# X by tokens from VectorE's 32 by 32 turns and a round trip through DRAM, in place of TensorE's transposes, in 13 of 14 chunks

## The chip, the cores and the metric

The program runs on one core of a Trainium2 chip. The metric is device microseconds (us) of one execution. Each comparison is made of several executions of both kernels, and their medians are compared; one more execution is taken by the hardware profiler, and all rows below come from it.

## The reference

Three layers follow each other: an attention with a sigmoid, a mixer with a low-rank token product and a two-layer channel product, and a second mixer. Only the last one is touched by the change. Cut to that:

```python
def _moe2_ref(x, w_theta, w_tok_r, w_tok_i, w_ch):   # x: 4 batches x 448 tokens x 768 features
    theta = x @ w_theta
    zr = x * np.cos(theta)
    zi = x * np.sin(theta)
    y = np.einsum('ts,bsd->btd', w_tok_r, zr) + np.einsum('ts,bsd->btd', w_tok_i, zi)
    u = x + y
    return u + np.maximum(u @ w_ch, 0.0)
```

## The kernel before

**Layout.** X lies in SBUF for the whole kernel as `X[P, NK, NT]`: 128 features on the partitions, 6 groups of features, 4 x 448 = 1792 tokens along the free axis. Each product is made of three matmuls on pairs of a high and a low part (`uh`/`ul`, `gh`/`gl`, `xh`/`xl`, `zh`/`zl`). The high part is a ScalarE copy, the low part a subtraction on VectorE (`lo_dve`, L119) or GpSimd (`lo_pool`, L113).

**The channel loop.** For `i` in 12 blocks of hidden channels and `b` in 4 batches, `ch1(i, b)` (36 matmuls of 448 columns) is followed by `ch2` of the pair before (three parts `e2`, 12 matmuls each). Behind each part VectorE adds the result `y` from PSUM to X (L690), and `y` has two PSUM buffers. `hook(i, b)` is called after each part, and runs one step of a conversion of a later weight (`tick`). The low part `gl` (L672) is also made by VectorE. The last block is `i == L` (11); in it a batch of X is complete after its third addition. In this block SyncE's queue also loads `tok` (the 3.1 MB of token weights, L749), the theta weights `th_r` (L236) that were kept in DRAM, and stores the last converted weights (L231).

**The theta stage.** The 1792 tokens are cut into 14 chunks of 128. For chunk `c`, `project` (L799, L800, L803) makes theta with tokens on the partitions in one of two PSUM buffers `th`; `trig` reduces it with two VectorE instructions (L819, L820) into the tile `t1`, and ScalarE makes sine and cosine in `t2` and `t1`, which have two buffers each. Since theta has tokens on the partitions, X is wanted with tokens on the partitions too. `natural` makes this: six TensorE transposes of 128 x 128 (L811) with the identity `ident` write one chunk of X into the PSUM tile `xn`. `zmake` (or `zmul` for the last chunk) multiplies it by sine and cosine on VectorE (L854, L856; L864, L865 in the two chunks that span two batches), then `zsplit` makes high and low parts, and the low parts are made by GpSimd for most chunks. `split_x` prepares `xh` and `xl` of the chunk after next, also with two buffers. `zmake` of one chunk stands in the middle of the next chunk's `project`. After chunks 4, 7 and 13 a `mix` of a batch follows (126 matmuls of 448 columns), whose `y` has two PSUM buffers that VectorE adds to X (L881).

**Order.** The schedule is manual: on each engine the instructions stand in the order in which the code issues them, and each engine runs its own in order. A DMA stands in the queue of the engine that issues it, and waits there for its data and its buffer. Buffers of a pool that are used again wait for their last reader.

Of the kernel before, what the change touches and what calls it, by code (L numbers as in the profile page):

```python
# [24 lines left out]
def tile_kernel(  # L25
# [59 lines left out]

    dpool = ctx.enter_context(tc.tile_pool(name="dpool", bufs=1, space=bass.MemoryType.DRAM))

    ident = cpool.tile([P, P], F32, name="ident")
    bias_s = cpool.tile([P, 1], F32, name="bias_s")
    half_pi = cpool.tile([P, 1], F32, name="half_pi")  # L90
    X = cpool.tile([P, NK, NT], F32, name="X")
# [9 lines left out]
    def pool(name, side="left", space=None):  # L101
        st = ExitStack()
        kw = dict(name=name, bufs=1, side=side, reuse_waits="tile")
        if space is not None:
            kw["space"] = space
        return st.enter_context(tc.tile_pool(**kw)), st
# [104 lines left out]

    kept = {}
    tok_d = dpool.tile([P, 2, NZ, S], F32, name="tok_d")

    def spill_tile(name):
        return late["sp"].tile([P, 2 * DM], F32, tag="sp", name=f"sp_{name}", bufs=1)
# [82 lines left out]
    ap, ap_st = pool("ap")  # L299
    ap1, ap1_st = pool("ap1")  # L300
    ap2, ap2_st = pool("ap2")
    ps_a, ps_a_st = pool("ps_a", "left", PSUM)
    ps_b, ps_b_st = pool("ps_b", "right", PSUM)
    u_in = ap.tile([P, 2, NS, R], F32, name="u_in")
# [407 lines left out]

    u23, u23_st = pool("u23")
    ps_y, ps_y_st = pool("ps_y", "left", PSUM)
    def hook(i, b):
        def after(e2):
            if (i, b) == (0, 1):
                ps = ps_g.tile([P, FB, 512], F32, tag="g", name=f"hl_{e2}", bufs=2)
                U2(B - 1, 2 * e2, ps, (vhl, vll))
            if i == 0 and b in (1, 2):  # L720
                split_u(b + 1, u23, 2 * e2, 2 * e2 + 2, lo_pool)
            tick(i, b, e2 + 2)
        return after
# [15 lines left out]
    for i in range(NB):  # L739
        for b in range(B):  # L740
            tick(i, b, 0)
            if (i, b) not in ((0, 0), (0, 1)):
                ch1(i, b)
            if i == L and b == 1:
                u01_st.close()
                tokhl, tokhl_st = pool("tokhl", "right")
                ctx.enter_context(tokhl_st)
                tok = tokhl.tile([P, 2, NZ, S], F32R, name="tok")
                nc.sync.dma_start(out=f(tok), in_=tok_d)  # L749
                tok_h, tok_l = tok[:, 0], tok[:, 1]  # L750
                xr, xr_st = pool("xr", "right")
                ctx.enter_context(xr_st)
            if i == L and b >= 2:
                split_x(b - 2)
            if i == L and b == 0:
                th_t[0] = load_kept("th0", "w1")
            if i == L and b == B - 1:
                th_t[2] = load_kept("th2", "w1")
                th_t[3] = load_kept("th3", "w1")
            if i == L and b == 1:  # L760
                th_t[1] = load_kept("th1", "w2")
            tick(i, b, 1)
            if prev is not None:
                ch2(*prev, hook(i, b))
            prev = (i, b)
            if (i, b) == (0, 1):
                uv_st.close()
                late["sp"], sp_st = pool("sp")
# [2 lines left out]
    th_t[4] = load_kept("th4", "w2")  # L771
    th_t[5] = load_kept("th5", "w2")
    sp_st.close()
    u23_st.close()
    gpool_st.close()
    cv_st.close()
# [26 lines left out]
                nc.tensor.matmul(ps[:, j, :HN], l[:, kk, :], wh[:, sl], start=False, stop=kk == NK - 1)  # L803
        return ps[:, :, :HN]

    def natural(c, name):

        ps = ps_e.tile([P, 2, 512], F32, tag="xn", name=f"{name}_{c}")
        for kk in range(NK):
            j, o = divmod(kk * P, HN)  # L810
            nc.tensor.transpose(ps[:, j, o:o + P], X[:, kk, c * P:(c + 1) * P], ident)  # L811
        return ps[:, :, :HN]

    def trig(c):

# [10 lines left out]
    def zsplit(key, t, lo):  # L826
        h = zp.tile([P, 2, HN], F32R, tag="zh", name=f"zh_{key[0]}_{key[1]}", bufs=12)
        l = zp.tile([P, 2, HN], F32R, tag="zl", name=f"zl_{key[0]}_{key[1]}", bufs=12)
        hi_act(h, t)
        lo(l, t, h)  # L830
        z_t[key] = (h.rearrange("p a n -> p (a n)"), l.rearrange("p a n -> p (a n)"))
# [4 lines left out]

    def zmul(c):
        cos, sin = T_t[c]
        xn = natural(c, "xn")
        nc.vector.tensor_mul(sin, xn, sin)  # L840
        nc.vector.tensor_mul(cos, xn, cos)

# [6 lines left out]
    def zmake(c):  # L849
        pr, ci, b, i = where(c)  # L850
        if ci != NFULL:
            cos, sin = T_t.pop(c)
            xn = natural(c, "xn")
            nc.vector.tensor_mul(sin, xn, sin)  # L854
            zsplit((b, NFULL + i), sin, lo_pool)
            nc.vector.tensor_mul(cos, xn, cos)  # L856
            zsplit((b, i), cos, lo_pool)
        else:
            cos, sin = T_t.pop(c)
            xn = natural(c, "xn")  # L860
            for n in range(2):
                t = zp.tile([P, 2, HN], F32, tag="zr", name=f"zr_{c}_{n}", bufs=2)
                sl = slice(n * REM, (n + 1) * REM)
                nc.vector.tensor_mul(t[REM:], xn[sl], sin[sl])  # L864
                nc.vector.tensor_mul(t[:REM], xn[sl], cos[sl])  # L865
                zsplit((2 * pr + n, 2 * NFULL), t, lo_pool if n else lo_dve)

    def mix(b, after=None):
        for d in range(NK):
# [12 lines left out]
            if after is not None:  # L882
                after(d)

    project(0, th_t, "th", 0, 4)
    project(1, th_t, "th", 0, 4)
    for c in range(NTC):
# [107 lines left out]
```

## Time and profile before

| what | value |
|---|---|
| median of 3 runs (lowest, highest) | 1170.18 us (1169.7, 1170.59) |
| the profiled execution, its own time | 1170.08 us |
| its span, first to last instruction | 1168.3 us |
| TensorE matmuls busy | 1155.3 us (99%) |
| VectorE, ScalarE, GpSimd busy | 647.9, 360.9, 189.5 us |
| mean granted TensorE clock | 0.998 |

Busy times are unions of an engine's instructions; matmuls overlap each other, so a busy TensorE is not one at its peak. In the rows of a timeline the first number is the start in us from the span's start, the second the duration, and a bracket at the end gives the idle time before it and who ended it. PE is TensorE, DVE is VectorE, ACT is ScalarE, POOL is GpSimd, SPq is the queue of SyncE.

### The profile page before, as it was taken

The numbers are of one execution on the slowest core, as the hardware profiler recorded it, in microseconds if no ns is written. First come the engines' busy times: TensorE is split into PE (matmuls) and PEld (weight loads), VectorE is DVE, ScalarE is ACT, GpSimd is POOL, SyncE is SP. The second block draws the span as 40 slices with busy tenths as digits, with TensorE's granted clock in tenths as the row PEclk, the third lists the DMA queues.
The fourth block names the chain that finished last, engine by engine and source line by source line (L and its number), as shares of the span: only waits on it lengthen the run. The fifth ranks groups of instructions, "written<-read, shape, count | busy, mean of one in ns | idle before, by whom it ended". The sixth has DMA issues, their size and how long they took to land.

```text
span 1168.3 us, 15638 instructions
## 1 busy us (share of the span) xinstructions
PE 1155.3 (99%) x6414; PEld 1000.5 (86%) x6414; DVE 647.9 (55%) x805; ACT 360.9 (31%) x465; POOL 189.5 (16%) x136
## 2 busy tenths in 40 slices
PE   7999999999999999999999999999999999999998
PEld 3444458999999999999999999999999999999997
DVE  4777873445554555455545556565375542732443
ACT  5878872212221222122212222222125341630110
POOL 2300012211111111111111122222002321410000
PEclk9999999999999999999999999999999999999999
DMA  9887830113231323132313242424431000120444
GB/s 168 165 162 141 161 83 1 55 54 97 51 133 54 97 52 131 54 97 53 130 54 98 66 140 61 155 61 156 164 138 52 1 1 1 45 119 1 61 64 66
DMA packets 183719, 100.57 MB, mean 86 GB/s; under 512 B 151232, under 2 KB 174656, under 8 KB 183520
## 3 DMA queue, kind: packets, MB, share of 16 engines
q1 hardware_dynamic: 156800, 87.95, 28.3%
q0 software_dynamic: 2368, 8.24, 2.5%
q10 hardware_dynamic: 24480, 3.39, 2.0%
q8 instruction: 50, 0.82, 0.3%
q14 instruction: 21, 0.17, 0.0%
HBM read 81.40 MB, written 18.15 MB: 85 GB/s over the span
## 4 chain that ended last, share of the span: by engine, by line
PE 97%; DMA 1%; SPq 1%; DVE 1%; ACT 0%; issue 0%; ACTq 0%
PE g L664 10%; PE g L666 10%; PE g L665 10%; PE y L686 10%; PE y L688 10%; PE y L687 10%; PE av L419 5%; PE sc L393 4%; PE y L877 3%; PE y L876 3%; PE y L878 3%; PE th L799 3%; PE th L803 3%; PE th L800 2%; PE wc L958 2%; PE wc L959 2%
## 5 line engine op out<-in xcount | busy, mean ns | idle before, releaser
L690 DVE TENSOR_TENSOR X<-y,X 128x896 f32<-128x896 f32 x144 | 157.1, 1091 | 114.9 <-PE y L688 113.5
L686 PE MATMUL y<-gh,w 128*128 128x448 f32 x576 | 210.7, 366 | 0.2 <-DVE X L690 0.2
L664 PE MATMUL g<-uh,w 128*128 128x448 f32 x576 | 210.7, 366 | 0.0
L687 PE MATMUL y<-gl,w 128*128 128x448 f32 x576 | 210.4, 365 | 0.0
L688 PE MATMUL y<-gh,w 128*128 128x448 f32 x576 | 210.4, 365 | 0.0
L666 PE MATMUL g<-uh,w 128*128 128x448 f32 x576 | 210.4, 365 | 0.0
L665 PE MATMUL g<-ul,w 128*128 128x448 f32 x576 | 210.4, 365 | 0.0
L671 ACT ACTIVATE gh<-g 128x896 fp32r<-128x896 f32 x48 | 44.1, 919 | 390.8 <-PE g L666 390.8
L672 DVE SCALAR_TENSOR_TENSOR gl<-g,gh 128x896 fp32r<-128x896 f32 x48 | 52.4, 1092 | 183.8 <-ACT gh L671 183.8
L113 POOL TENSOR_TENSOR w<-ca_w,w 128x768 fp32r<-128x768 f32 x42 | 77.8, 1853 | 432.0 <-ACT w L110 432.0
L664 PEld LDWEIGHTS g<-uh,w 128*128 128x128 f32 x576 | 108.2, 188 | 9.8 <-ACT uh L110 0.7
L686 PEld LDWEIGHTS y<-gh,w 128*128 128x128 f32 x576 | 108.2, 188 | 9.7 <-issue 1.1
L688 PEld LDWEIGHTS y<-gh,w 128*128 128x128 f32 x576 | 108.2, 188 | 8.6
L666 PEld LDWEIGHTS g<-uh,w 128*128 128x128 f32 x576 | 108.2, 188 | 8.6
L687 PEld LDWEIGHTS y<-gl,w 128*128 128x128 f32 x576 | 108.2, 188 | 8.6
L665 PEld LDWEIGHTS g<-ul,w 128*128 128x128 f32 x576 | 108.2, 188 | 8.5
L384 ACT ACTIVATE A<-sc,bias_s 128x896 f32<-128x896 f32 x72 | 72.2, 1006 | 23.4 <-PE sc L393 12.8
L419 PE MATMUL av<-A,v 128*64 128x448 f32 x288 | 65.2, 561 | 0.0
L876 PE MATMUL y<-tok,zh 128*128 128x448 f32 x168 | 61.7, 367 | 0.0
L877 PE MATMUL y<-tok,zh 128*128 128x448 f32 x168 | 61.5, 366 | 0.0
L113 POOL TENSOR_TENSOR zl<-t,zh 128x768 fp32r<-128x768 f32 x23 | 42.7, 1880 | 115.4 <-ACT zh L110 115.4
L878 PE MATMUL y<-tok,zl 128*128 128x448 f32 x168 | 61.4, 366 | 0.0
(139 smaller groups left out, 1634.6 us busy)
## 6 DMA issues: line engine op xcount, KB each, us to landing
ws_w<-in_moe_w_ch_dram SPq DMA_DIRECT2D x40, 768.0 KB, 4.4
ws_w<-in_moe_w_ch_dram POOLq DMA_DIRECT2D x8, 768.0 KB, 5.9
k<-in_k_dram SPq DMA_DIRECT2D x94, 56.0 KB, 2.7
q<-in_q_dram SPq DMA_DIRECT2D x93, 56.0 KB, 3.1
ws_th<-in_moe_w_theta_dram SPq DMA_DIRECT2D x6, 768.0 KB, 4.3
th_d<-sp_th SPq DMA_DIRECT2D x6, 768.0 KB, 4.1
ws_wc<-in_moe_w_ch_dram SPq DMA_DIRECT2D x6, 768.0 KB, 4.7
wc_d<-sp_wc SPq DMA_DIRECT2D x6, 768.0 KB, 4.5
```

The lines of the kernel that those rows point to most:

```text
L113: nc.gpsimd.tensor_sub(o, a, b)
L419: nc.tensor.matmul(ps[h * D:(h + 1) * D, :S], v_t[p // 2][:, 2 * (p % 2) + h, c, :], A_t[p, c][:, h, :], start=c == 0 and p % 2 == 0, stop ...
L664: nc.tensor.matmul(o, wh[:, sl], uh_t[b][:, kk, :], start=kk == 0, stop=False)
L665: nc.tensor.matmul(o, wh[:, sl], ul_t[b][:, kk, :], start=False, stop=False)
L666: nc.tensor.matmul(o, wl[:, sl], uh_t[b][:, kk, :], start=False, stop=kk == NK - 1)
L686: nc.tensor.matmul(o, wh[:, sl], gh[:, j, :], start=j == 0, stop=False)
L687: nc.tensor.matmul(o, wh[:, sl], gl[:, j, :], start=False, stop=False)
L688: nc.tensor.matmul(o, wl[:, sl], gh[:, j, :], start=False, stop=j == FB - 1)
L690: nc.vector.tensor_add(x, ps[:, :, :S], x)
L876: nc.tensor.matmul(o, zh[:, sl], tok_h[:, i, :], start=n == 0, stop=False)
L877: nc.tensor.matmul(o, zh[:, sl], tok_l[:, i, :], start=False, stop=False)
L878: nc.tensor.matmul(o, zl[:, sl], tok_h[:, i, :], start=False, stop=n == NZ - 1)
```

## The change

The transposes leave TensorE for chunks 0 to 12. In their place each batch of X, once complete, is turned by VectorE in squares of 32 by 32 (`turn_x`: one instruction for 128 features x 448 tokens), stored in this form to a DRAM tensor `x_d`, and later loaded with the squares set in their places (`load_xn`: four DMAs for each chunk, each of 32 partitions x 24 pieces of 32 floats) into an SBUF tile of the tag `zr`, which now has three buffers. Batches 0 to 2 are turned in the last block of the channel loop, two turns behind each part of `ch2`, through three staging buffers `stg`. Batch 3 is turned after the loop, through the buffers of `t1` and `t2`. Chunks 0 and 1 are loaded ahead of these last turns, each other chunk from two `zmake`s ahead of it on. The last chunk keeps TensorE's transposes, with an identity that GpSimd makes anew. The first `ident` moves into a pool that is closed earlier.

```diff
-    ident = cpool.tile([P, P], F32, name="ident")
...
+    x_d = dpool.tile([DM, NT], F32, name="x_d")
...
+    ident = ap2.tile([P, P], F32, name="ident")
...
+    def turn_x(b, d, t):
+        nc.vector.transpose(out=t, in_=X[:, d, b * S:(b + 1) * S])
+        nc.sync.dma_start(out=x_d[d * P:(d + 1) * P, b * S:(b + 1) * S], in_=t)
+
     def hook(i, b):
         def after(e2):
+            if i == L and 0 < b < B:
+                for d in (2 * e2, 2 * e2 + 1):
+                    turn_x(b - 1, d, late["stg"].tile([P, S], F32, tag="stg", name=f"stg_{b}_{d}", bufs=3))
...
-    def natural(c, name):
-
-        ps = ps_e.tile([P, 2, 512], F32, tag="xn", name=f"{name}_{c}")
-        for kk in range(NK):
-            j, o = divmod(kk * P, HN)
-            nc.tensor.transpose(ps[:, j, o:o + P], X[:, kk, c * P:(c + 1) * P], ident)
-        return ps[:, :, :HN]
+    xn_t = {}
+
+    def load_xn(c):
+        t = xn_t[c] = zp.tile([P, 2, HN], F32, tag="zr", name=f"xn_{c}", bufs=3)
+        for a in range(P // R):
+            o = c * P + a * R
+            nc.sync.dma_start(
+                out=t[a * R:(a + 1) * R].rearrange("i a (g j) -> i (a g) j", j=R),
+                in_=x_d[:, o:o + R].rearrange("(g i) j -> i g j", i=R),
+            )
+
+    def natural(c):
+
+        ip = zp.tile([P, 2, HN], F32, tag="zr", name="ident_r", bufs=3).rearrange("p a n -> p (a n)")[:, :P]
+        make_identity(nc, ip)
...
-            xn = natural(c, "xn")
+            xn = xn_t.pop(c)
...
+            load_xn(c + 1)
+        _, second, _, _ = where(c + 1)
+        if c + 2 < NTC - 1 and second != NFULL:
+            load_xn(c + 2)
+        elif c + 2 == NTC - 1:
+            xn_t[c + 2] = natural(c + 2)
...
+    load_xn(0)
+    load_xn(1)
+    for d in range(NK):
+        tag = f"t{d % 2 + 1}"
+        t = zp.tile([P, 2, HN], F32, tag=tag, name=f"stg_{B}_{d}", bufs=2).rearrange("p a n -> p (a n)")[:, :S]
+        turn_x(B - 1, d, t)
     project(0, th_t, "th", 0, 4)
```

VectorE, last block of the channel loop, from the second part of `ch2(11, 0)` to the first of `ch2(11, 1)`. Before:

```order
L690 TENSOR_TENSOR X<-y_0_1_6653,X 128x2x448
L151 SCALAR_TENSOR_TENSOR ws_th_6389<-ca_th_6636,ws_th_6389 128x768
L690 TENSOR_TENSOR X<-y_0_2_6668,X 128x2x448
L157 SCALAR_TENSOR_TENSOR ca_th_6636<-ca_th_6636,ws_th_6389 128x768
L672 SCALAR_TENSOR_TENSOR gl_2_6721<-g_2_6683,gh_2_6720 128x896
L119 TENSOR_TENSOR xl_0_6725<-X,xh_0_6724 128x768
L690 TENSOR_TENSOR X<-y_1_0_6730,X 128x2x448
```

And now:

```order
L691 TENSOR_TENSOR X<-y_0_1_6663,X 128x2x448
L717 STREAM_TRANSPOSE stg_2_6677<-X 128x448
L717 STREAM_TRANSPOSE stg_3_6680<-X 128x448
L150 SCALAR_TENSOR_TENSOR ws_th_6390<-ca_th_6640,ws_th_6390 128x768
L691 TENSOR_TENSOR X<-y_0_2_6684,X 128x2x448
L717 STREAM_TRANSPOSE stg_4_6698<-X 128x448
L717 STREAM_TRANSPOSE stg_5_6701<-X 128x448
L156 SCALAR_TENSOR_TENSOR ca_th_6640<-ca_th_6640,ws_th_6390 128x768
L673 SCALAR_TENSOR_TENSOR gl_2_6743<-g_2_6705,gh_2_6742 128x896
L118 TENSOR_TENSOR xl_0_6747<-X,xh_0_6746 128x768
L691 TENSOR_TENSOR X<-y_1_0_6752,X 128x2x448
```

Each addition now has two turns behind it, and from the fourth on a turn needs a staging buffer whose store must have landed.

SyncE's queue, in the same block (its first rows) and around the end of the loop (its last). In `ws_wc` and `ws_th` lie weights on their way to conversion. Before:

```order
L749 DMA tok<-tok_d 128x6272
L236 DMA th_r<-th_d 128x1536
L194 DMA ws_wc_6634<-in_moe_w_ch_dram 128x1536
L231 DMA th_d<-sp_th_6744 128x1536
L236 DMA th_r<-th_d 128x1536 x2
L231 DMA th_d<-sp_th_6846 128x1536
L231 DMA wc_d<-sp_wc_6897 128x1536
L236 DMA th_r<-th_d 128x1536 x2
```

And now, at these two places:

```order
L757 DMA tok<-tok_d 128x6272
L236 DMA th_r<-th_d 128x1536
L193 DMA ws_wc_6638<-in_moe_w_ch_dram 128x1536
L718 DMA x_d<-stg_0_6656 128x448
L718 DMA x_d<-stg_1_6659 128x448
L718 DMA x_d<-stg_2_6677 128x448
```

```order
L231 DMA wc_d<-sp_wc_6955 128x1536
L236 DMA th_r<-th_d 128x1536 x2
L822 DMA xn_7008<-x_d 32x24x32 x4
L822 DMA xn_7013<-x_d 32x24x32 x4
L718 DMA x_d<-stg_0_7018 128x448
L718 DMA x_d<-stg_1_7021 128x448
L718 DMA x_d<-stg_2_7024 128x448
```

The first stores stand right behind `tok`, `th_r` and `ws_wc`; the stores of batch 3 stand behind the last two `th_r` and the eight loads of chunks 0 and 1.

VectorE, from the last addition of the loop to `trig(0)` (L819, now L845). Before:

```order
L690 TENSOR_TENSOR X<-y_3_1_6900,X 128x2x448
L690 TENSOR_TENSOR X<-y_3_2_6916,X 128x2x448
L819 TENSOR_SCALAR t_0_7014<-th_6949 128x768
L820 TENSOR_TENSOR t_0_7014<-th_6949,t_0_7014 128x768
L119 TENSOR_TENSOR xl_2_7012<-X,xh_2_7011 128x768
```

And now:

```order
L691 TENSOR_TENSOR X<-y_3_2_6974,X 128x2x448
L717 STREAM_TRANSPOSE stg_0_7018<-X 128x448
L717 STREAM_TRANSPOSE stg_1_7021<-X 128x448
L717 STREAM_TRANSPOSE stg_2_7024<-X 128x448
L717 STREAM_TRANSPOSE stg_3_7027<-X 128x448
L717 STREAM_TRANSPOSE stg_4_7030<-X 128x448
L717 STREAM_TRANSPOSE stg_5_7033<-X 128x448
L845 TENSOR_SCALAR t_0_7101<-th_7036 128x768
L846 TENSOR_TENSOR t_0_7101<-th_7036,t_0_7101 128x768
L118 TENSOR_TENSOR xl_2_7099<-X,xh_2_7098 128x768
```

Six turns now stand ahead of `trig(0)`; the first four fill both buffers of `t1` and `t2`, and the last two use the first two again.

## Rows read from the trace of the kernel before

**Rows 1.** The page: the chain that ended last, shares of the span by engine.
```profile
PE 97%; DMA 1%; SPq 1%; DVE 1%; ACT 0%; issue 0%; ACTq 0%
```

**Rows 2.** Timeline of TensorE around the six transposes of chunk 0.
```profile
891.23 0.82 PE L811 MATMUL xn<-ident,X 128*128 128x128 f32 x6
891.80 0.43 PE L799 MATMUL th<-th_r,xh 128*128 128x384 f32 x1
892.07 0.34 PE L800 MATMUL th<-th_r,xh 128*128 128x384 f32 x1
892.24 0.33 PE L799 MATMUL th<-th_r,xh 128*128 128x384 f32 x1
```

**Rows 3.** Timeline of VectorE in the last block of the channel loop.
```profile
833.48 1.09 DVE L690 TENSOR_TENSOR X<-y,X 128x896 f32<-128x896 f32 x1 [0.33 <-PE y L688]
...
835.92 1.09 DVE L690 TENSOR_TENSOR X<-y,X 128x896 f32<-128x896 f32 x1 [0.87 <-PE y L688]
...
846.60 1.09 DVE L672 SCALAR_TENSOR_TENSOR gl<-g,gh 128x896 fp32r<-128x896 f32 x1 [6.29 <-ACT gh L671]
...
848.47 1.08 DVE L690 TENSOR_TENSOR X<-y,X 128x896 f32<-128x896 f32 x1
849.47 0.95 DVE L176 SCALAR_TENSOR_TENSOR ws_th<-ca_th,sp_th 128x768 f32<-128x768 f32 x1
...
851.80 1.09 DVE L690 TENSOR_TENSOR X<-y,X 128x896 f32<-128x896 f32 x1
...
875.39 1.09 DVE L690 TENSOR_TENSOR X<-y,X 128x896 f32<-128x896 f32 x1 [1.39 <-PE y L688]
```

**Rows 4.** Timeline of VectorE: two turns of the output, the form that is added.
```profile
1090.80 1.17 DVE L929 STREAM_TRANSPOSE o<-X 128x448 f32<-128x448 f32 x2
```

**Rows 5.** Timeline of TensorE in the last block: the one wait for VectorE.
```profile
867.68 0.44 PE L686 MATMUL y<-gh,w 128*128 128x448 f32 x1 [0.20 <-DVE X L690]
```

**Rows 6.** DMA issues from 831 to 832.5: count, KB each, us to landing.
```profile
tok<-tok_d SPq DMA_DIRECT2D x1, 3136.0 KB, 10.3
th_r<-th_d SPq DMA_DIRECT2D x1, 768.0 KB, 11.8
ws_wc<-in_moe_w_ch_dram SPq DMA_DIRECT2D x1, 768.0 KB, 13.1
```

**Rows 7.** Timeline of SyncE's queue: two issues.
```profile
831.41 0.43 SPq L236 DMA_DIRECT2D th_r<-th_d  x1
831.97 0.35 SPq L194 DMA_DIRECT2D ws_wc<-in_moe_w_ch_dram  x1
```

**Rows 8.** SyncE's issues of four loads in 128-byte pieces, and the DMA packets from 28 to 33.
```profile
28.44 1.98 SPq L318 DMA_DIRECT2D k<-in_k_dram  x4
...
DMA packets 4413, 0.66 MB, mean 132 GB/s; under 512 B 4351, under 2 KB 4381, under 8 KB 4413
...
q1 hardware_dynamic: 4306, 0.53, 65.9%
```

**Rows 9.** Timelines of GpSimd and VectorE in the theta stage.
```profile
894.61 7.25 POOL L113 TENSOR_TENSOR zl<-t,zh 128x768 fp32r<-128x768 f32 x4 [21.44 <-ACT zh L110]
...
885.80 0.96 DVE L819 TENSOR_SCALAR t<-th 128x768 f32<-128x768 f32 x1 [9.31 <-PE th L803]
...
896.81 0.95 DVE L856 TENSOR_TENSOR t<-xn,t 128x768 f32<-128x768 f32 x1
898.29 0.96 DVE L819 TENSOR_SCALAR t<-th 128x768 f32<-128x768 f32 x1 [0.53 <-POOL zl L113]
...
900.16 2.52 DVE L119 TENSOR_TENSOR xl<-X,xh 128x768 fp32r<-128x768 f32 x1
...
917.50 0.61 DVE L881 TENSOR_TENSOR X<-y,X 128x448 f32<-128x448 f32 x1
```

**Rows 10.** The granted clock (third from last) in a stretch, and TensorE's wait ahead of it.
```profile
27.20:30.60 3.40, 3.40 (x14) 1.85 (x14) 3.07 (x7) 1.88 (x3) 0.55 (x2) 0.50 0.66 108
...
26.16 0.97 PE L402 MATMUL sl<-qT,kT 64*64 64x448 f32 x4 [1.77 <-DVE qT L354]
```

More of the change, by code (lines that the diff above doesn't have):

```diff
@@ L752, in tile_kernel @@
                 ctx.enter_context(xr_st)
+                late["stg"], stg_st = pool("stg", "right")
             if i == L and b >= 2:
@@ L773, in tile_kernel @@
     sp_st.close()
+    stg_st.close()
     u23_st.close()
@@ L804, in project, with turn @@
         return ps[:, :, :HN]
-    def natural(c, name):
-        ps = ps_e.tile([P, 2, 512], F32, tag="xn", name=f"{name}_{c}")
-        for kk in range(NK):
-            j, o = divmod(kk * P, HN)
-            nc.tensor.transpose(ps[:, j, o:o + P], X[:, kk, c * P:(c + 1) * P], ident)
-        return ps[:, :, :HN]
+    xn_t = {}
[10 more added lines that the diff above has]
+        make_identity(nc, ip)
+        def turn():
+            ps = ps_e.tile([P, 2, 512], F32, tag="xn", name=f"xn_{c}")
+            for kk in range(NK):
+                j, o = divmod(kk * P, HN)
+                nc.tensor.transpose(ps[:, j, o:o + P], X[:, kk, c * P:(c + 1) * P], ip)
+            xn_t[c] = ps[:, :, :HN]
+        return turn
     def trig(c):
@@ L838, in zmul @@
         cos, sin = T_t[c]
-        xn = natural(c, "xn")
+        xn_t[c]()
+        xn = xn_t.pop(c)
         nc.vector.tensor_mul(sin, xn, sin)
@@ L852, in zmake @@
             cos, sin = T_t.pop(c)
-            xn = natural(c, "xn")
+            xn = xn_t.pop(c)
             nc.vector.tensor_mul(sin, xn, sin)
@@ L859, in zmake @@
             cos, sin = T_t.pop(c)
-            xn = natural(c, "xn")
+            xn = xn_t.pop(c)
             for n in range(2):
-                t = zp.tile([P, 2, HN], F32, tag="zr", name=f"zr_{c}_{n}", bufs=2)
+                t = zp.tile([P, 2, HN], F32, tag="zr", name=f"zr_{c}_{n}", bufs=3)
                 sl = slice(n * REM, (n + 1) * REM)
```

## The prediction

> **What bounds the kernel now.** I read first the page's chain of work that ended last: 97% of the span is TensorE [rows 1], so time is won only by taking instructions from TensorE or by ending its waits, and a change elsewhere costs whatever TensorE then waits. Second, the timeline of TensorE around one `natural`, to see what the transposes cost in place [rows 2]. Third, the timelines of VectorE, SyncE and GpSimd at the places where the new work lands, because there the question is how much room is left [rows 3 to 9]. In the last block of the channel loop VectorE has little: from 846.60 to 851.80 seven instructions follow each other without a gap [rows 3], and TensorE already waits once for an addition, 0.2 us [rows 5].
>
> **Removed: 13 x 6 transposes.** The six start at 891.23 and the next matmul at 891.80, 0.57 us; the matmul after that follows 0.27 later, where 0.17 is normal, which adds 0.09 [rows 2]. So 0.66 us for a chunk, all of it on TensorE's path, 13 x 0.66 = **8.6 us gained**. The first `ident` moves to another pool and nothing waits for that: 0. The identity made anew is two GpSimd instructions between subtractions whose results are wanted two batches of `mix` later: 0, and at most some tenths.
>
> **Added in the last block: 18 turns and stores (B).** Two turns take 1.17 us [rows 4], and start when the addition ahead of them has ended. I carry the order forward with the rows' starts. A part of `ch2` is 2.44 us (833.48 to 835.92), three parts or one `ch1` 7.3 us; an addition, `gl` or two turns hold VectorE 1.0 to 1.1 us, `xl` and the conversion steps 0.9, the short step 0.5 [rows 3, 4].
>
> The first trouble is a landing. The turn of group 3 needs the staging buffer of group 0, so store 0 must have landed. It is issued near 835.2, right behind `tok`, `th_r` and `ws_wc`. `th_r` (768 KB) is issued 0.4 us after `tok` and lands 11.8 us later, after `tok` has landed: these transfers come one after the other, not side by side [rows 6]. `ws_wc` lands at 831.97 + 13.1 = 845.1, 1.8 us behind `th_r` (831.41 + 11.8) [rows 6, 7]. A store of 224 KB takes 0.53 us at that pace and lands at 845.6, where VectorE would have wanted it at 837.9. Queued behind the waiting turn: the step L151, then the third addition (847.0 to 848.1), two turns, L157, `gl`, `xl`, and the first addition of `ch2(11, 1)` at 851.9 to 853.0 (before: 848.47). TensorE's third part there could start at 850.4 and needs this addition's PSUM buffer: it starts at 853.0, **2.6 us late**.
>
> From there VectorE is simply too full. The next additions end at 857.5, 860.6, 866.8, 871.3, 874.4 and 877.5. TensorE, at 862.8 for `ch2(11, 2)`, does three parts freely, then waits for 871.3 (1.2 us), 874.4 (0.7) and 877.5 (0.7), and ends at 879.9 instead of about 875.3, the start of the last addition before [rows 3]. The waits come to 5.2 us, less the one there already was, and the end moves by **4.6 us**. If the store did not wait for the large transfers, 2.0 would be left; more than 5.2 has no reason. I take 4.6.
>
> **Added at the end of the loop: batch 3 and the first loads (C).** VectorE turns groups 0 to 3 from 881.0 to 883.2 into the buffers of `t1` and `t2`. Group 4 uses the first buffer again and waits until store 0 of this batch has landed, and `trig(0)` (L819, L820) stands behind group 5 in VectorE's order. In SyncE's queue these stores stand behind the last `wc_d`, two `th_r` and eight loads of chunks 0 and 1. `wc_d` is issued near 879.2 (its data is now ready later, by VectorE's lag). The three large transfers move in 3 x 1.83 = 5.5 us, and with the 2.8 us that `tok` shows beyond its moving time (10.3 less 3136/768 x 1.83 = 7.5 [rows 6]) the second `th_r` lands at 887.5, just ahead of TensorE's need at 888 to 889: no wait. The loads are 2 x 4 x 768 = 6144 pieces of 128 bytes. No row shows this load; the nearest are the loads of k and q in the same pieces: 4413 packets in 5 us, with the queue busy 65.9% [rows 8]. So 6144 pieces take between 4.6 us (if the queue were full) and 7.0 us (at that pace); SyncE needs 0.52 us for each such load of 448 pieces (four fill 1.98 us and the gap behind), thus 4.2 to 7.1 us for eight. Store 0 lands at 892.1 to 894.6, then two turns and the two instructions of `trig(0)` (3.0 us) end at 895.1 to 897.6. TensorE, with chunks 0 and 1 projected (72 matmuls of 0.174 us) from 879.9, wants that PSUM buffer at 892.4: a wait of 2.7 to 5.2. I take **3.9**, the middle; the ends of the bounds are 0, if the stores land freely, and 5.2.
>
> **Moved in the theta stage: the multiplication's operand (D).** Before, `xn` came from PSUM; now from SBUF, beside `t` in SBUF. The rows show what GpSimd does to a VectorE instruction with two SBUF operands: `xl` (X and `xh`) starts at 900.16 under GpSimd's fourth subtraction, which ends at 894.61 + 7.25 = 901.86, and takes 2.52 us instead of 0.95, ending 0.8 after GpSimd; the multiplication with `xn` in PSUM at 896.81 runs under GpSimd in 0.95 [rows 3, 9]. I count from p, the end of `trig(0)`. `trig(2)` needs GpSimd's second subtraction, which reads the tile whose buffer it takes; before, it started at 898.29 as that ended [rows 9], and 885.80 + 1.95 = 887.75 was p, so p + 10.5. Now the fourth multiplication waits for the first subtraction and the second subtraction for this multiplication, 0.8: p + 11.3, and `trig(2)` ends at p + 13.3. TensorE wants it for chunk 4 at p + 12.5 (two chunks of 6.25 without transposes): 0.8. `xl` of chunk 4 then waits for GpSimd's fourth subtraction and ends at p + 15.8, and TensorE wants it at p + 14.0: 1.8. Last, `mix` of batch 0: the first addition ended at 918.11 [rows 9], and between it and the third tile of `y`, which needs its buffer, TensorE still had the transposes of chunk 4 to do, 0.57 us that now go; with two more waits for GpSimd of up to 1.8 ahead of that addition I put 1.3 there, between 0 and 2. Later stretches are followed by a `mix` that gives time back. Together **3.9 us**; if only subtractions wait and multiplications do not, the second subtraction keeps its place and 2.0 are left. I take 3.9, since the multiplication is the same instruction with its operands in the same places as `xl`.
>
> The Trainium skill, SBUF — State Buffer, section "Who interferes with whom", says that a VectorE instruction with two SBUF inputs and a GpSimd instruction that reads SBUF exclude each other for the whole instruction. By it D is 3.9 and the sum +3.8; by the narrow reading of the rows, subtractions alone, 2.0 and +1.9. The trace agrees for `xl` (2.52 us) and shows no such multiplication.
>
> **Sum.** -8.6 + 4.6 + 3.9 + 3.9 = **+3.8 us**. The profiled execution took 1170.08 us (its span 1168.3, 1.8 around it), the median of the runs is 1170.18, so they stand for each other: 1170.1 + 3.8 = **1173.9 us**, slower by 0.3%.
>
> **Rivals.**
> 1. *The stores overtake* (faster). If a small store lands without waiting for the transfers issued ahead of it, B is 2.0, everything behind is 2.6 earlier, store 0 of batch 3 lands some 2.6 us after its issue (`tok_d`, or any unloaded transfer here, has about that beside its moving time [rows 6]) and C is about 0.3: -8.6 + 2.0 + 0.3 + 3.9 = -2.4, with D at 2.0 -4.3; 1165.8 to 1168.5, say **1167.0**. It decides if store 0 lands before about 841. Against it stands `th_r` at 11.8 us [rows 6]; for it, that these were all large. The Trainium skill, DMA: Bandwidth & Descriptors, section "Queues, rings and completion order", says that completion is not first-in-first-out per issuing engine, though each engine takes descriptors in ring order; by its first half this rival, by its second the forecast. The trace agrees with the second half (11.8 us).
> 2. *Small prices* (no change). The multiplications do not wait for GpSimd (D 2.0) and the loads run at the quick bound (C 2.7): -8.6 + 4.6 + 2.7 + 2.0 = +0.7, **1170.8**; with either alone 1172.0 to 1172.7.
> 3. *The pause is worse.* The pieces of `x_d` lie further apart than those of k, so loads at one and a half times the slow bound add 3.5 us; and TensorE stands still for 4 us or more. Before, the clock was granted at 0.50 (1.2 GHz) for 3.4 us right after a wait of 1.77 us in sparse work [rows 10]; that would cost up to 1.7 us more, part of it hidden under D. -8.6 + 4.6 + 7.4 + 3.9 + 1 = +8.3, **1178.4**.
>
> **How the numbers follow.** Forecast (1172.6 to 1176.5) 0.50, rival 3 0.12, rival 2 0.25, rival 1 0.13. A difference under 0.2% (2.3 us, 1167.8 to 1172.5) is about what cannot be told from no change. So slower 0.62, same 0.25, faster 0.13. The range for 8 in 10 takes in rival 1's middle and rival 3's: 1167.0 to 1179.0.
>
> **What would show it.** B: a turn in the last block that starts only after `ws_wc` has landed, near 845, and TensorE waiting for L691 three or four times, 4 to 5 us in all; wrong if store 0 lands near 838. C: TensorE waits 3 to 5 us for L846 at the third projection, and `t` for a landing of `x_d`; wrong if there is no wait. D: multiplications (L881) that take 2 us and more under GpSimd's subtractions, and waits of one or two us at the projection of chunk 4 and in the first `mix`. The projections themselves should run 0.66 us shorter for each chunk; from the second `mix` on the lag should shrink. The prediction is wrong as a whole if the `th` stage starts less than 2 us later than before.

## The result and the profile after

The changed kernel takes 1179.0 us (median of six, 1177.1 to 1180.4) against 1170.2 for the kernel before (1169.1 to 1170.8): a ratio of 1.0075, 95% interval 1.0065 to 1.0086. It is slower by 8.9 us, where 3.8 were forecast. Its profiled execution took 1180.3 us.

The page's chain that ended last has VectorE, DMA and SyncE's queue in it now, where TensorE held nearly all of it [rows 1]:

```profile
PE 87%; DVE 5%; DMA 4%; SPq 2%; issue 1%; ACT 1%; POOL 0%; ACTq 0%; DVEq 0%
```

TensorE's waits from the last block to the first `mix` (timeline of TensorE; start, duration, and in the bracket the wait and who ended it). Before there was one, of 0.20 [rows 5]:

```profile
849.74 0.47 PE L687 MATMUL y<-gh,w 128*128 128x448 f32 x1 [0.65 <-DVE X L691]
854.65 0.47 PE L687 MATMUL y<-gh,w 128*128 128x448 f32 x1 [2.21 <-DVE X L691]
874.86 0.44 PE L687 MATMUL y<-gh,w 128*128 128x448 f32 x1 [1.37 <-DVE X L691]
877.81 0.47 PE L687 MATMUL y<-gh,w 128*128 128x448 f32 x1 [0.28 <-DVE X L691]
880.86 0.47 PE L687 MATMUL y<-gh,w 128*128 128x448 f32 x1 [0.31 <-DVE X L691]
...
900.90 0.66 PE L809 MATMUL th<-th_r,xh 128*128 128x384 f32 x1 [4.84 <-DVE t L846]
...
917.85 0.62 PE L813 MATMUL th<-th_r,xl 128*128 128x384 f32 x2 [0.79 <-DVE xl L118]
933.84 0.47 PE L909 MATMUL y<-tok,zh 128*128 128x448 f32 x1 [1.39 <-DVE X L914]
```

The first five are B (4.8 us in all), the 4.84 is C, the last two belong to D. All but the first, of 0.65, stand where the prediction had put a wait; the wait of 0.8 for `trig(2)` that it had in D did not come here. VectorE shows the causes, in its timeline; the rows answer [rows 3] and [rows 9]:

```profile
847.20 0.65 DVE L717 STREAM_TRANSPOSE stg<-X 128x448 f32<-128x448 f32 x1 [8.25 <-DMA x_d<-stg]
847.76 0.92 DVE L150 SCALAR_TENSOR_TENSOR ws_th<-ca_th,ws_th 128x768 uint32<-128x768 uint32 x1
848.60 1.08 DVE L691 TENSOR_TENSOR X<-y,X 128x896 f32<-128x896 f32 x1
...
897.67 1.19 DVE L717 STREAM_TRANSPOSE stg<-X 128x448 f32<-128x448 f32 x2 [10.85 <-DMA x_d<-stg]
898.80 0.96 DVE L845 TENSOR_SCALAR t<-th 128x768 f32<-128x768 f32 x1
899.80 0.96 DVE L846 TENSOR_TENSOR t<-th,t 128x768 f32<-128x768 f32 x1
...
909.06 2.60 DVE L883 TENSOR_TENSOR t<-xn,t 128x768 f32<-128x768 f32 x1
913.40 0.96 DVE L845 TENSOR_SCALAR t<-th 128x768 f32<-128x768 f32 x1 [1.74 <-POOL zl L112]
...
915.27 2.53 DVE L118 TENSOR_TENSOR xl<-X,xh 128x768 fp32r<-128x768 f32 x1
```

The fourth turn waits 8.25 us for store 0, the fifth of batch 3 waits 10.85 us for its store, and one multiplication with both operands in SBUF takes 2.60 us beside GpSimd's subtractions, where the three ahead of it take 0.95.

What the prediction did not have in its sum is the clock. Busy times by stretch (length; PE, PEld, DVE, ACT, POOL busy with counts; granted TensorE clock; DMA share; GB/s):

```profile
855.69:859.10 3.41, 3.41 (x11) 3.04 (x10) 3.38 (x5) 0.00 (x0) 0.00 (x0) 0.50 0.39 139
...
900.06:906.89 6.83, 5.99 (x19) 6.02 (x20) 4.70 (x6) 5.96 (x7) 0.00 (x0) 0.50 0.43 77
```

Twice the clock is granted at 0.50, the lower of its two levels (1.2 GHz): 1.0 us behind the wait of 2.21 us, and from 0.8 us before the end of the wait of 4.84 on. In the second stretch nineteen matmuls of 384 columns take 5.99 us; at full clock they are 3.3 (0.174 each).

To compare kernels without the noise of their first 830 us (the last block begins between 830.2 and 832.8 in most profiled runs, also in kernels whose edit lies behind it), I cut each trace at the first matmul of `ch2(11, 0)`, at the first of the theta stage, and at the end of the kernel's last matmul. Before, then after (the part from the theta stage on is cut once more, at the first matmul of chunk 5):

```profile
830.85:875.20 44.35, 44.15 (x218) 40.49 (x217) 26.73 (x29) 8.92 (x11) 1.84 (x1) 1.00 0.50 191
875.20:935.84 60.64, 60.59 (x337) 57.95 (x336) 32.23 (x34) 26.38 (x31) 17.15 (x9) 1.00 0.09 32
935.84:1162.60 226.76, 226.76 (x1189) 213.76 (x1187) 99.85 (x149) 56.77 (x76) 29.31 (x16) 1.00 0.22 45
```

```profile
831.89:883.39 51.50, 46.67 (x217) 41.51 (x216) 36.69 (x47) 9.18 (x11) 1.85 (x1) 0.97 0.62 235
883.39:950.97 67.58, 60.57 (x308) 57.41 (x306) 38.41 (x40) 26.27 (x31) 17.94 (x9) 0.95 0.48 103
950.97:1173.06 222.09, 221.65 (x1141) 208.65 (x1139) 102.47 (x149) 56.43 (x76) 30.29 (x18) 1.00 0.28 54
```

The last block is 7.15 us longer, chunks 0 to 4 with the first `mix` 6.94 longer, and what follows 4.67 shorter: +9.4 in all (the block also begins 1.0 later, which lies ahead of the edits). The gain comes only in the third stretch; in the second it is more than eaten up.

### The profile page after: what moved, and what is told of

It is laid out like the page before. It is cut to its first block, busy times and chain, and to the rows that moved or that the text cites. A ratio compares the mean times of both kernels' runs of the same rounds, so it can differ in the third digit from the quotient of the medians.

```text
span 1178.5 us, 15645 instructions
## 1 busy us (share of the span) xinstructions
PE 1153.6 (98%) x6336; PEld 995.9 (85%) x6336; DVE 667.1 (57%) x829; ACT 360.3 (31%) x465; POOL 190.9 (16%) x138
## 4 chain that ended last, share of the span: by engine, by line
PE 87%; DVE 5%; DMA 4%; SPq 2%; issue 1%; ACT 1%; POOL 0%; ACTq 0%; DVEq 0%
PE g L665 10%; PE g L666 10%; PE g L667 10%; PE y L687 9%; PE y L689 9%; PE y L688 9%; PE av L420 4%; PE sc L394 3%; PE y L909 3%; PE y L910 3%; PE y L911 3%; PE wc L996 2%; PE wc L998 2%; PE wc L997 2%; DMA q<-in_q_dram 2%; PE th L813 1%
## 5 line engine op out<-in xcount | busy, mean ns | idle before, releaser
L909 PE MATMUL y<-tok,zh 128*128 128x448 f32 x168 | 61.6, 367 | 1.4 <-DVE X L914 1.4
L809 PE MATMUL th<-th_r,xh 128*128 128x384 f32 x168 | 57.5, 342 | 4.8 <-DVE t L846 4.8
```

What stands on the lines that cost most here:

```text
L909: nc.tensor.matmul(o, zh[:, sl], tok_h[:, i, :], start=n == 0, stop=False)
```

## The experiments

All differences are to the kernel before in the same comparison (1171.0 to 1171.4 us there). "Block" is the first stretch and "rest" the two behind it together, 44.35 and 287.40 us before, 51.50 and 289.67 after.

**The gain with the operand still in PSUM.** In the kernel before, `natural`:

```diff
+        if 0 < c < NTC - 1:
+            return xn_k[0]
```

> The kernel before with the transposes of chunks 1 to 12 left out: their multiplications read the PSUM tile of chunk 0, so the output is not the reference's. It measures the gain alone, with the operand still in PSUM. My theory: 12 x 0.66 = 7.9 us less than before (1170.2), 1162.3; up to 2.0 of it given back where GpSimd's subtractions and VectorE now set the pace of the theta stage, so 1162.3 to 1164.3. Rival (the transposes cost less in place than 0.66, since the stage is paced by VectorE and GpSimd anyway): 1165 or more.

Measured: 1166.6 us, 4.6 less (ratio 0.9959, 0.9948 to 0.9971). The rest is 282.21 us, 5.19 less than before, so 2.7 of the 7.9 are given back, more than the 2.0 that the theory allowed: by its time this is the rival. Its reason does not hold: where nothing waits (chunks 9 to 12), the projection of a chunk starts 6.91 us after the one before it in the kernel before and 6.24 here, so a chunk's transposes do cost 0.67 in place. But TensorE waits 0.66 for `xl`, 0.91 for the first addition of the first `mix` and 0.43 for a later `xl`: without the transposes it catches up with VectorE and GpSimd.

**Gain and D together.** The same, with the operand in SBUF:

```diff
+        if c < NTC - 1:
+            return f(tok_h[:, 0:2, :HN])
```

> The kernel before with the transposes of chunks 0 to 12 left out and their multiplications reading a piece of tok in SBUF (values that have nothing to do with X, so the output is not the reference's); no turns, stores or loads are added. It measures the gain and term D together. My theory as forecast: -8.6 + 3.9 = 1165.5. By the waits seen in the changed kernel's trace (0.8, 1.4 and 0.4 us) D is 2.2 to 2.6: 1163.8 to 1164.2. Rival, only subtractions wait for GpSimd: 2.0 or less, at most 1163.6, and the multiplications take 0.95 us under GpSimd, not 2.4 to 2.6.

Measured: 1167.7 us, 3.4 less (0.9970, 0.9960 to 0.9980); rest 283.48, which is 3.92 less. So gain and D make -3.9 where the prediction had -4.7; the waits of the changed kernel's trace had let me expect more gain than that, not less. Against the run above the rest is 1.27 longer although one chunk more goes without transposes (0.66): the operand in SBUF costs 1.9 us, just the 3.9 less 2.0 of the prediction. VectorE's and GpSimd's timelines of this run:

```profile
895.74 0.95 DVE L856 TENSOR_TENSOR t<-tok,t 128x768 f32<-128x768 f32 x1
896.61 2.61 DVE L858 TENSOR_TENSOR t<-tok,t 128x768 f32<-128x768 f32 x1
900.96 0.96 DVE L821 TENSOR_SCALAR t<-th 128x768 f32<-128x768 f32 x1 [1.75 <-POOL zl L113]
```

```profile
896.48 8.03 POOL L113 TENSOR_TENSOR zl<-t,zh 128x768 fp32r<-128x768 f32 x4 [21.43 <-ACT zh L110]
```

GpSimd's first subtraction begins at 896.48, between the two: one multiplication takes 0.95 us without it, the other 2.61 under it. Of the 32 multiplications of the stage three take over 1.3 us here (2.61, 2.45, 1.57), each begun under a subtraction, and none with the operand in PSUM. The Trainium skill, SBUF — State Buffer, section "Who interferes with whom", says that a VectorE instruction with two SBUF inputs contends with a GpSimd instruction that reads SBUF; the trace agrees, and now for multiplications too.

**B alone.** The kernel before with the 18 turns and stores of batches 0 to 2, in the changed kernel's place:

```diff
+            if i == L and 0 < b < B:
+                for d in (2 * e2, 2 * e2 + 1):
+                    turn_x(b - 1, d, late["stg"].tile(..., bufs=3))
```

> The kernel before (1170.2 to 1171.2 in the runs so far) with term B alone: the 18 turns and stores of batches 0 to 2 in the last block, which nobody reads; the transposes stay. Forecast of the prediction: +4.6. From the changed kernel's trace: the stretch from ch2(11,0) to the theta stage took 51.5 us against 44.4, +7.1, with a stretch at half clock in it, and +5.9 in the run of e3 whose clock did not fall there. So +5.9 with the clock whole, +7.1 with the fall. Rival, the theta stage behind it gives part back, since VectorE and GpSimd pace it: +3 to +5.

Measured: 1178.2 us, +7.2 (1.0059, 1.0047 to 1.0071). Its profiled run, the fastest at 1176.8:

```profile
831.78:881.67 49.89, 45.10 (x217) 40.18 (x216) 36.68 (x47) 9.16 (x11) 1.85 (x1) 1.00 0.64 242
881.67:1169.10 287.43, 287.38 (x1525) 271.74 (x1523) 132.06 (x183) 83.14 (x107) 46.48 (x25) 1.00 0.20 44
```

The block is 5.54 longer and the rest is as before: nothing is given back. The five waits are those of the changed kernel (0.59, 2.21, 1.36, 0.28, 0.34), but this time the clock stays at 1.00, and the block is 1.6 shorter than the changed kernel's. So B is 5.5 with its waits, and 1.6 more if the clock falls.

**C alone.** The kernel before with batch 3's turns and stores behind eight loads:

```diff
+    for c in range(2):
+        t = zp.tile([P, 2, HN], F32, tag="zr", name=f"xn_{c}", bufs=2)
...
+    for d in range(NK):
...
+        nc.vector.transpose(out=t, in_=X[:, d, (B - 1) * S:B * S])
+        nc.sync.dma_start(out=x_d[d * P:(d + 1) * P, (B - 1) * S:B * S], in_=t)
```

> The kernel before with term C alone: batch 3's six turns and stores through the buffers of t1 and t2 behind the eight loads of chunks 0 and 1, which nobody reads; the transposes stay, and x_d is filled with six plain stores in block 5, where SyncE's queue is idle. Forecast: +3.9 (2.7 to 5.2). By the changed kernel's trace the wait for trig(0) is 4.8, which with a stretch of half clock behind it makes +6 to +8. Rival, a fall of the clock behind the wait is paid by work that would have waited for VectorE and GpSimd: +4 to +5, with a 0.50 in the granted clock or without.

Measured: 1177.2 us, +6.2 (1.0056, 1.0041 to 1.0070). The profiled run lost 6 us long before the edit, so it is read by stretches alone: block 44.33, rest 293.34, +5.94. The wait, and the clock around it:

```profile
897.62 0.66 PE L803 MATMUL th<-th_r,xh 128*128 128x384 f32 x1 [3.55 <-DVE t L824]
```

```profile
896.29:903.12 6.83, 5.50 (x17) 5.53 (x18) 4.79 (x6) 6.48 (x8) 0.00 (x0) 0.50 0.12 46
903.12:920.00 16.88, 16.88 (x107) 16.75 (x107) 12.63 (x13) 11.43 (x15) 11.67 (x6) 1.00 0.01 1
```

From the last matmul ahead of the wait to the first behind it 3.89 us pass, 0.17 is normal: the wait costs 3.7. The other 2.2 I put down to the half clock: 17 matmuls in 5.50 us instead of 3.0 (2.5 by these; the 0.3 between is not resolved). Behind them there is no wait in which the loss could hide, so here it is paid whole.

**The wait of C taken away.** The changed kernel with the loads behind batch 3's stores:

```diff
-    load_xn(0)
-    load_xn(1)
     for d in range(NK):
...
         turn_x(B - 1, d, t)
+    load_xn(0)
+    load_xn(1)
```

> The changed kernel (1179.0) with batch 3's six turns and stores issued ahead of the eight loads of chunks 0 and 1 in SyncE's queue. My theory: the 4.8 us that TensorE waits for trig(0) go down to at most 0.5, and the stretch at half clock behind it (6.8 us at 0.50, some 3 us lost) goes with it: 1179.0 - 4.5 - 3 = 1171.5. Rival 1, the clock at 0.50 costs nothing that other waits would not have cost: 1174.2 to 1174.7. Rival 2, the wait only moves, since store 0 still stands behind the last two th_r and the loads now come later for the first multiplication: 1177 or more.

Measured: 1175.8 us, +4.6 (1.0050, 1.0037 to 1.0063), so 4.3 better than the changed kernel and not 7.5. TensorE's timeline:

```profile
896.38 0.41 PE L809 MATMUL th<-th_r,xh 128*128 128x384 f32 x1 [0.45 <-DVE t L846]
910.17 0.41 PE L809 MATMUL th<-th_r,xh 128*128 128x384 f32 x1 [0.95 <-DVE t L846]
912.48 0.80 PE L813 MATMUL th<-th_r,xl 128*128 128x384 f32 x2 [1.37 <-DVE xl L118]
```

The wait of 4.84 shrinks to 0.45 as expected. But D's waits, 0.79 behind C in the changed kernel, are 0.95 and 1.37 now, and behind them the clock is granted at 0.50 from 912.75 to 916.16. My expectation had taken the three costs for independent; the time gained is rival 1's. In the traces the rest is 284.93, 4.7 shorter than the changed kernel's. The block, which this edit does not touch, is 1.3 shorter too (50.24): it has the wait of 2.21, but the clock did not fall behind it this time. Four of the six runs took 1175.2 to 1175.8 us, two 1179.5 and 1179.7.

**The standing still taken away, the wait kept.** The changed kernel with dummy matmuls where TensorE waits for C:

```diff
+            if c == 2:
+                fill = ps_e.tile([P, 2, 512], F32, tag="xn", name="fill")
+                for n in range(22):
+                    nc.tensor.matmul(fill[:, n % 2, :HN], xs_t[1][0][:, 0, :], ...)
```

> The changed kernel (1179.0) with 22 matmuls of 384 columns more, into a PSUM tile that nobody reads, between the projections of chunks 1 and 2, where TensorE waits 4.8 us for trig(0). They take 22 x 0.174 = 3.8 us, so they do not lengthen the wait. My theory, the clock falls because TensorE stood still: the 6.8 us at 0.50 there are gone and the time is 3 us shorter, 1176. Rival, the clock's fall there costs nothing (what follows is held by VectorE and GpSimd anyway) or does not hang on the wait: 1179.0 or, if the fill is late, up to 1180.

Measured: 1182.7 us, +11.5 (1.0093, 1.0080 to 1.0106): not 3 less but 2.7 more than the changed kernel; in the traces the rest is 290.93, 1.3 more. The first half of my theory held: the clock stays at 1.00 from 884 to 917. But TensorE then arrives earlier at D's waits, 1.79 and 1.33, and there the clock falls:

```profile
915.84 0.41 PE L809 MATMUL th<-th_r,xh 128*128 128x384 f32 x1 [1.79 <-DVE t L846]
918.12 1.01 PE L813 MATMUL th<-th_r,xl 128*128 128x384 f32 x2 [1.33 <-DVE xl L118]
```

```profile
900.00:917.00 17.00, 13.86 (x77) 13.04 (x76) 13.04 (x13) 12.09 (x15) 7.73 (x4) 1.00 0.35 62
917.16:923.99 6.83, 5.87 (x18) 5.87 (x19) 6.71 (x7) 5.89 (x8) 4.19 (x3) 0.50 0.00 1
```

In the changed kernel, then, the slow stretch behind C covers part of D's waits. The rival was nearer than my theory, but neither had a loss of 2.7 in it; 1.3 of it stands in the rest, and the other 1.4 shows in no row.

**Batch 0's stores from ScalarE's queue.** The changed kernel with

```diff
-        nc.sync.dma_start(out=x_d[...], in_=t)
+        (nc.scalar if b == 0 else nc.sync).dma_start(out=x_d[...], in_=t)
```

> The changed kernel (1179.0) with the six stores of batch 0 issued from ScalarE's queue instead of SyncE's, where tok, th_r and ws_wc stand ahead. My theory, the order within one queue holds store 0 back until 847.2: from another queue it lands 2 to 3 us after its issue, the third part of ch2(11,1) is not late, the 2.2 us wait of TensorE and the half clock behind it go: 1174 to 1176.5. Rival, the DMA engines themselves are full with the large transfers whatever the queue: store 0 lands at 843 or later and the time is 1178 to 1179.5.

Measured: 1176.8 us, +5.8 (1.0052, 1.0039 to 1.0065). DMA issues from 835 to 835.7 (count, KB each, us to landing), and the turn that needs this store:

```profile
x_d<-stg ACTq DMA_DIRECT2D x1, 224.0 KB, 8.7
```

```profile
844.04 0.65 DVE L717 STREAM_TRANSPOSE stg<-X 128x448 f32<-128x448 f32 x1 [6.08 <-DMA x_d<-stg]
```

The expectation had paired the time and the landing wrongly: the time is near my theory's, the landing is the rival's. The store still needs 8.7 us, so the order in SyncE's queue is not all that holds it: the transfers in flight do so from another queue too. It lands 3.2 us earlier than in the changed kernel (844.0, 847.2); 1.0 of that is the earlier start of the block, and `ws_wc`, which landed ahead of it there, is issued only at 841.9 here. The Trainium skill, DMA: Bandwidth & Descriptors, section "Queues, rings and completion order", says that both issuing engines' queues run on the same 16 DMA engines, which agrees; it also says that these take turns between queues, by which a small store would land ahead of `tok` (841.8); here it landed behind `tok`, though ahead of `th_r` (844.96), which was issued 3.9 us before it. The block is 48.46 us, 3.0 shorter than the changed kernel's: the wait of 0.65 is gone, the next is shorter, and the clock stays at 1.00.

```profile
852.15 0.47 PE L687 MATMUL y<-gh,w 128*128 128x448 f32 x1 [1.63 <-DVE X L691]
```

**A version without B and C.** No turns in the loop. Batches 0 and 1 are turned in the 9 us behind it in which VectorE is idle [rows 9], batch 2 in the first `mix`, batch 3 in the second. Once with the low parts as in the changed kernel, once with those of the cosine products of chunks 0 to 2 moved from GpSimd to VectorE, behind `trig`:

```diff
+    for b in range(2):
+        for d in range(NK):
+            turn_z(b, d)
     load_xn(0)
     load_xn(1)
...
+                late_lo.append(zsplit((b, i), cos, lambda l, t, h: (l, t, h)))
...
+        while late_lo:
+            lo_dve(*late_lo.pop(0))
```

> The version of best2 with all cosine low parts left to GpSimd as in the changed kernel; nothing else differs from best2. It tells what GpSimd's subtractions cost beside multiplications with two SBUF operands. My theory (they hold VectorE's multiplications up, 2.4 to 2.6 us each instead of 0.95): slower than best2 (5.5 us under the kernel before) by about the 1.9 us by which e2 and e1 differ, so 3 to 4 us under the kernel before, 1167 to 1168. Rival, the port price is hidden by now: the same as best2 within 0.7.

> A version meant to be faster than both: X by tokens from VectorE's turns as in the changed kernel, but no turns in the channel loop. Batches 0 and 1 are turned in the 9 us behind it in which VectorE is idle, through buffers of zh and zl that are still free, with their stores ahead of the loads; batch 2 is turned in the first mix and batch 3 in the second; and the low parts of the cosine products of chunks 0 to 2 are made by VectorE behind trig instead of GpSimd. By my theory B and C are gone, and what is left is the gain and a smaller D: e2 (gain with D) was 3.4 us under the kernel before, so 1167.7 less up to 2 of its 3.5 us of waits, 1165.7 to 1167.7. Rival, the loads or the batch 0 and 1 stores come too late for the first multiplication and TensorE waits for them: 1169 to 1172.

Measured: 1167.7 us, 3.7 less than before (0.9971, 0.9961 to 0.9981), and 1165.5, 5.5 less (0.9955, 0.9943 to 0.9967); rest 284.10 and 282.49. Without B and C the change gains what gain and D leave (3.4 above), and taking GpSimd off three products brings 1.8 more. In chunks 0 to 4 the first version has multiplications of 2.59 and 2.42 us and an `xl` of 2.52 beside GpSimd's subtractions, the second none of them over 1.9. But TensorE's waits add up to nearly the same in both (2.85 and 2.57 us); most of the 1.6 between their rests is a half-clock stretch, which the first version has behind a pair of waits (1.11 and 1.40) and the second does not:

```profile
905.74:909.15 3.41, 3.41 (x12) 3.41 (x11) 3.38 (x4) 3.03 (x4) 2.47 (x2) 0.50 0.02 5
```

Twelve matmuls of 384 columns take 3.41 us there instead of 2.1. So the 1.8 is not the price of the shared access by itself.

**Mends at the waits that were left.** The loads of chunks 0 and 1 ahead of batch 1's stores, four PSUM buffers for `mix`, and in the chunk that spans two batches (`zr`) all multiplications ahead of the low parts:

```diff
-    load_xn(0)
-    load_xn(1)
+        if b == 0:
+            load_xn(0)
+            load_xn(1)
...
-            ps = ps_e.tile([P, 512], F32, tag="y", name=f"y2_{b}_{d}", bufs=2)
+            ps = ps_e.tile([P, 512], F32, tag="y", name=f"y2_{b}_{d}", bufs=4)
...
+                zr.append(t)
+            for n, t in enumerate(zr):
                 zsplit(...)
```

> best2 with three mends at the waits that its trace still shows for TensorE (0.54 for trig(2), whose chunk 1 multiplication waited for its load; 0.32 for zl; 1.39 for the first addition of the first mix; 0.32 for xl): chunks 0 and 1 are loaded ahead of batch 1's stores, the four multiplications of the chunk that spans two batches come ahead of its low part, and mix has four PSUM buffers instead of two (the last chunk's transposes go to one of th's). My theory: each wait lost about 0.15 more than it shows, 3.2 in all; 2 to 3 of them go: 8 us under the kernel before, 1163 (1162.5 to 1164). Rival, the waits move on to the next addition or the next low part: 5.5 to 6.5 under, 1164.5 to 1165.5.

Measured: 1166.5 us, 4.9 less (0.9957, 0.9944 to 0.9969): the rival's waits that move on, and less gain than either had, though the rest is 281.74, 0.8 shorter than the version before it. The wait for the first addition is gone, and 1.39 us stand at the low part that one mend had moved back. So this one was undone:

```diff
-                zr.append(t)
-            for n, t in enumerate(zr):
                 zsplit(...)
```

> best3 with one of its three mends undone: in the chunk that spans two batches the first low part stands again behind the first two multiplications, not behind all four. In best3's trace TensorE waits 1.39 for that low part in the first mix, where best2 waited 0.32 for it and then 1.39 for the first addition; with four PSUM buffers the second wait should stay away. My theory: the stretch from the theta stage to the last matmul, 282.5 us in best2 and 281.7 in best3, becomes 280.6 to 280.9, about 1 us less than best3, 6 us under the kernel before. Rival: the addition is late all the same and the wait comes one tile later, 281.5 or more.

Measured: 1164.6 us, 6.6 less than before (0.9943, 0.9929 to 0.9956); rest 280.84, as expected. TensorE's waits in chunks 0 to 4 and the first `mix`:

```profile
902.11 0.41 PE L804 MATMUL th<-th_r,xh 128*128 128x384 f32 x1 [0.50 <-DVE t L841]
...
913.31 0.47 PE L914 MATMUL y<-tok,zl 128*128 128x448 f32 x1 [0.32 <-DVE zl L118]
```

Of the 8.6 us that the transposes take, 6.6 are had here, with three low parts on VectorE, two more PSUM buffers and the loads moved besides the turns. The kernel before has no wait of TensorE in the theta stage, so these mends had none to end there; they were not run on it by themselves.

## Why the prediction was right in direction and short by five

| term | prediction | measured alone | where |
|---|---|---|---|
| gain and D | -8.6 + 3.9 = -4.7 | -3.9 | rest, operand in SBUF |
| B | +4.6 | +5.5 with waits; +1.6 clock (not alone) | block, B alone; after less B alone |
| C | +3.9 | +3.7 wait, +2.2 clock | rest, C alone |
| sum | +3.8 | +9.1 | after, both stretches: +9.4 |

The 1.6 is taken from the changed kernel's own block, so the block agrees by construction; the test is the rest, where -3.9 and +5.9 make +2.0 and +2.3 is measured. Even there two differences offset each other: the wait of C is 4.84 in the changed kernel and 3.55 alone, D's waits 2.6 in all and 3.5 without B and C. By the medians the three runs make -3.4 + 7.2 + 6.2 = +10.0 against +8.9. So nothing large is missing, to about 1 us. The measured 1179.0 lies above the forecast's own band (1172.6 to 1176.5) and at the very end of the range for 8 in 10.

**The gain** was right in price (0.66 a chunk; 0.67 measured) but, as the first run shows, D is more than the operand's place: 2.7 us are given back with the operand in PSUM, 4.7 with it in SBUF (8.6 less 3.9). The share of that place, 1.9, is the prediction's. The three waits that it named came at 0.42, 1.38 and 1.31 where it had 0.8, 1.8 and 1.3; the total is larger all the same, by a `xl` wait in chunk 13 (0.43 in the trace) and by restarts: a wait of 1.38 in the row moves the next matmul by 1.55, and the one behind it by 0.1 more.

**B**: right in place and mechanism, 0.9 short in its waits. Store 0 landed at 847.2 and not at 845.6; 1.0 of that is the later start of the block. The issues of the changed kernel from 831 to 837 (count, KB each, us to landing) answer [rows 6]:

```profile
tok<-tok_d SPq DMA_DIRECT2D x1, 3136.0 KB, 10.2
th_r<-th_d SPq DMA_DIRECT2D x1, 768.0 KB, 11.6
ws_wc<-in_moe_w_ch_dram SPq DMA_DIRECT2D x1, 768.0 KB, 13.5
x_d<-stg SPq DMA_DIRECT2D x1, 224.0 KB, 10.8
```

The store landed behind all three, as forecast. What the order carried forward did not show is the wait of 0.65 for the third addition, ahead of the one of 2.21, and the restarts.

**C**: right in mechanism and within the bounds, with some luck in the size. The wait is 4.84 in the changed kernel and costs 3.7 alone. The loads ran near the quick end (the eight landed from 892.88 to 897.10, 0.60 us apart, estimated 0.58 to 0.88), for which the prediction had 2.7. The rest of the 4.84 is elsewhere: the second `th_r` landed at 892.31, 9.4 us after the issue of `wc_d` at 882.88 and not 8.3; store 0 landed at 897.58, 0.5 behind the last load; and 0.3 more passed on VectorE. While `th_r` moved, SyncE's queue stood still at loads, one issue taking 3.67 us, so the stores were issued from 894.57 on only. Whether an earlier issue alone would have landed them earlier is not shown. The issue of the fourth load:

```profile
888.36 3.67 SPq L822 DMA_DIRECT2D xn<-x_d  x1
```

**The step that failed** is the clock. The prediction had read the row at 0.50 behind a wait of 1.77 us [rows 10], but put the fall into rival 3 alone, at 12 in 100 and with 1 us, as a peculiarity of sparse work. In the profiled runs it came in dense work too: behind 2.21 us in two of the four traces that have this wait, at each of the waits of 3.6, 4.8 and 4.9 us, and behind pairs of shorter waits close together (1.8 and 1.3, 1.0 and 1.4, 1.1 and 1.4), though not behind 0.4 and 1.4. By the runs of single terms it is worth 1.6 at B and 2.2 at C, 3.8 of the 5.3 that the sum was short; the other 1.5 are B's waits (+0.9) and gain and D (+0.8), less 0.2 at the wait of C. That the fall costs 2.2 at C in the changed kernel too is not shown: with the wait filled the clock did not fall there, and TensorE waited for D instead. Over the six runs of the changed kernel the time goes with the mean granted clock: 1177.1 and 1177.8 us at 0.996, 1178.6 to 1180.3 at 0.995, 1180.4 at 0.994. A mean lower by 0.002 is 2.4 us of lost work in 1178; 2.9 is seen; the means are rounded to 0.001, and take in the whole kernel, so this agrees and proves little.

**The rivals.** Overtaking stores (1) fell: 10.8 us to landing, where an undisturbed store takes 1.9 to 2.1 (the rival had 2.6). Small prices (2) fell at the multiplications, though the loads did run quick. Rival 3 gave 1178.4, near the time, but by other parts: its slow loads did not come, its clock came twice and larger. Its sum also had a slip: the 3.5 for slow loads are counted from the slow end of C (5.2) but were added to the middle (3.9); from the slow end it is 1179.7.

**What stays open**: why the same 2.21 us in B was followed by the half clock in the profiled runs of the changed kernel and of the filled one, and not in those of B alone and of the stores put first; the five runs of B alone all have a mean clock of 0.997 to 0.998. And their median lies 1.4 above the profiled run with no wait that I could name for it, so the size of B itself is known to about 1.5 us only.

## What to carry to other kernels

Taking work from the bounding engine pays only where the others have the room: the same edit costs 8.9 us with its turns in a full VectorE and its stores behind large transfers, and gains 3.7 with both moved to idle stretches, 6.6 with the waits that were left mended too. Ask of every wait that a change adds to TensorE what a half-clock stretch behind it would cost (here 1.3 to 2.7 us, and it came at two of the four waits of 2.21 us and at all three from 3.6 us up), and then whether later waits cover it, since removing one stall lets the engine run into the next. Test terms alone, in the kernel before, and check that they add up, with no term taken from the whole itself.

## What was not expected of the hardware

- A small store issued from another engine's queue was still slow beside the large transfers in flight: 8.7 us to landing for 224 KB, behind 3.1 MB and ahead of 768 KB that were issued before it, against a median of 2.0 over the 24 stores of the changed kernel.
- An issue held SyncE's queue for 3.67 us with large transfers ahead of it; the stores' issues in the same queue took 0.3 to 0.6.
- A VectorE multiplication with both operands in SBUF took up to 2.61 us beside a GpSimd subtraction and 0.95 with one operand in PSUM, but only three of 32 took over 1.3.
- The granted clock fell to 0.50 in dense matmul work, around waits of 2.2 to 4.9 us or pairs of shorter ones, for stretches of 3.41 or 6.83 us, and a filled wait moved the fall 17 us on instead of ending it.
